# Query/key tiles as head pairs in every batch, and a new division into chunks

## The chip, the cores and the metric

One NeuronCore of a Trainium2 chip runs the whole program. The metric is the device time of one execution in microseconds, the median of several. The engines run side by side, each through its own instructions in order: PE (TensorE, matrix products, with PEld for its weight loads), DVE (VectorE), ACT (ScalarE), POOL (GpSimd) and SP (SyncE, whose queue issues the transfers). They wait for each other through semaphores.

## What is computed

Banded attention, then a feed-forward block, then a soft mixture of experts, all in float32. Shapes: q, k and v are 4 batches x 8 heads x 768 positions x 64; the rows that follow are 3072 x 512.

```python
def _attn_ref(q, k, v, n_global, n_local):          # 8 global keys, 96 local ones
    scores = scale * np.matmul(q, k.transpose(0, 1, 3, 2))
    ...
    scores = np.where(keep, scores + bias, -1e9)
    a = softmax(scores); return np.matmul(a, v)

def _moe_ref(x, w_in, w_out):                        # 512 -> 2048 -> 512
    h = x @ w_in
    return (h * (1.0 / (1.0 + np.exp(-h)))) @ w_out

def _moe2_ref(x, phi, w1, w2):                       # 8 experts, 4 slots each
    logits = x @ phi
    slot_input = softmax(logits, axis=0).T @ x
    ...
    return softmax(logits, axis=1) @ slot_out
```

## The kernel before

**Numbers in two halves.** Each float32 operand is split into a high and a low float16 part: `hi` (line 189) scales and rounds, `lo` (line 197) subtracts the high part from the input (lines 199 and 201 are its two forms). A product is then three: high x high, high x low, low x high.

**Tiles and chunks.** The 3072 rows are 24 tiles T of 128, six to a batch. `CHUNKS` (line 33) groups them, eight chunks of three. For a chunk c the feed-forward block runs as 16 calls of `l1_step` (line 453, 12 products of 384 columns each at lines 460 to 462, then Tanh on ACT at 464, a DVE multiply at 466 and the split of the result), and then `l2_part` and `l2_end` (lines 475 and 484, 48 products of 512 columns for each tile at lines 480 to 482, then the logits and the transposed copies). Behind a chunk follow `logits`, `slots1`, `slots2` and `slots3` (lines 497 to 555), the running softmax over all rows; L518, L528 and L548 are their products on PE. Each is put off by some slots with `at` (line 224): `lag_s` is 2.

**Attention.** `load(T)` (line 240) brings a tile's q, k and v through SP's queue into one staging buffer. `split(T)` (line 247) makes the halves: engine letters in `HE` and `HLO` choose who does it; from tile 6 on POOL does the high parts and DVE the low ones. `s_step(T, pr)` (line 272) takes heads 2pr and 2pr+1: scores on PE (line 293), mask and row maximum on DVE (298), exponential on ACT (299); after every second step the weights of four heads are split and transposed by a DMA (314). `pv_step(T, half)` (line 324) multiplies them by v (336) and scales (344 to 346).

There are two layouts for q and k, chosen by `paired(T)` (line 236), which is `T < NPAIR`, the first batch:
- Tiles 0 to 5 use `q_f` and `k_f`: 128 partitions hold two heads of 64, four such pairs side by side. The score of a head is three products over 64 rows, (high, high), (high, low), (low, high), and each head has its own PSUM bank. A split handles 128x512 elements.
- Tiles 6 to 23 use `q_l` and `k_l`: each head's 64 rows stand twice, one above the other, eight heads side by side. The high part of q stands in the upper 64 rows, its low part in the lower ones. A score is two products over 128 rows, with the high and with the low part of k. Both heads of a step share one bank, and the two banks of `bS` alternate from step to step. A split handles 128x1024 elements for k, and 64x1024 for the low part of q.

```python
h, r, terms = (pr, slice(64 * i, 64 * i + 64), ((0, 0), (0, 1), (1, 0))) if paired(T) else (2 * pr + i, slice(0, 128), ((0, 0), (0, 1)))
```

**Order.** `first_items` (line 358) runs the attention of chunk 0's tiles. After that chunk c's feed-forward work and the attention of chunk c+1 are interleaved: `other_items` (line 377) lists the attention calls, and `upto` marks how far a chunk must get. Each l1 step, and each quarter of a tile in l2, ends with `slot_end` (line 764), which runs the delayed work that is due and as many attention items as are proportional to the slots passed, over 16 + 4n - 5 slots for a chunk of n tiles. Chunk 0 has 28 slots in all and 29 items; it also carries the weight conversions `conv(p)` (line 414), eight for w_in ahead of the l1 steps that need them and eight for w_out in l2 (DVE at lines 421, 429, 430 and 448, ACT at 428 and 440, POOL at 426 and 446). A conversion's weights come through six places in SBUF, filled by `w_ahead` (line 407) on SP's queue when a place is free. The last chunk has no attention beside it and takes its own path (`last_part` and what follows), then come the expert layers and the output. The build sorts the instructions of an engine by when it expects them to be ready, so the order in the trace is near the code's but not the same.

Of the kernel before, what the change touches and what calls it, by code (L numbers as in the profile page):

```python
# [9 lines left out]
F32 = mybir.dt.float32  # L10
# [6 lines left out]
B, H, S, D = 4, 8, 768, 64  # L17
DM, DFF = 512, 2048
# [6 lines left out]
F16 = mybir.dt.float16  # L25
# [5 lines left out]
NTILE = NT // 128  # L31
TPB = S // 128
CHUNKS = [3, 3, 3, 3, 3, 3, 3, 3]
NCH = len(CHUNKS)
# [5 lines left out]
E_QK, E_V, E_WI, E_WO, E_G, E_X2, E_PHI, E_E = 0, 15, 16, 17, 14, 14, 13, 12  # L40
# [48 lines left out]
BE = 'A'  # L89
NPAIR = 6  # L90
HLO = 'VPVVVV'
# [8 lines left out]

def fast_kernel(tc, keepp, q_l, k_l, v_l, q_f, k_f, n_global, n_local, w_in, w_out, phi, w1, w2, shapes, pick_c, out):


    nc = tc.nc
    V, A, G = nc.vector, nc.scalar, nc.gpsimd
    mm = nc.tensor.matmul
# [3 lines left out]
    with ExitStack() as ctx:  # L110
# [4 lines left out]
        ar = Arena(pool.tile([128, NB // 4], F32, name="arena"), NB)  # L115
# [4 lines left out]
        bS, bPV, bW, bM = bank[0:2], bank[2], bank[3:7], bank[7]  # L120
# [38 lines left out]
        g0 = ar.off  # L159
# [75 lines left out]

        def paired(T):

            return T < NPAIR

        def load(T, bufs):  # L240
            if paired(T):
                bufs = [bufs[0][:, 0:4], bufs[1][:, 0:4], bufs[2]]
            for s, src in zip(bufs, (q_f, k_f, v_l) if paired(T) else (q_l, k_l, v_l)):
                nc.sync.dma_start(out=s, in_=src[T])
            staged[T] = bufs

        def split(T):
            qs, ks, vs = staged.pop(T)
            t, u = T % TPB, T % NR
            he = HE[T] if T < len(HE) else "P"  # L250
            le = HLO[T] if T < len(HLO) else "V"
            qd = q16[T % 2]
            n = 4 if paired(T) else 8
            if paired(T):
                qh, ql, qf = qd[:, 0:4], qd[:, 4:8], qs
            else:
                qh, ql, qf = qd, qd[64:128], qs[64:128]
            hi(he, qh, qs, E_QK)
            lo("P" if le == "P" else "V", ql, qf, E_QK, qh if paired(T) else ql)
            hi(he, kr[:, 0, 0:n, u], ks, E_QK)  # L260
            lo("V" if le == "V" else "P", kr[:, 1, 0:n, u], ks, E_QK, kr[:, 0, 0:n, u])
            v3 = vs.rearrange("p (h d) -> p h d", h=H)
            hi(he, v16[:, u, :, 0], v3, E_V)
            lo("V", v16[:, u, :, 1], v3, E_V, v16[:, u, :, 0])
            if t == 0:
                hi("P", kg[:, :, 0:n], kr[:, :, 0:n, u, 0:8], 0)
            if T == 0:
                hi("P", vg[0:8], v16[0:8, u], 0)
            if t == 2:
                absmax(T // TPB, v16[:, u, 0:2, 0], AX.XY)  # L270

        def s_step(T, pr):
            t, u = T % TPB, T % NR
            w = 128 if t == 0 else 256
            half, lp = pr // 2, pr % 2
            if paired(T):
                sp = [bS[i][:, 256 * (pr % 2):256 * (pr % 2) + 256] for i in range(2)]
            else:
                sp = [bS[pr % 2][:, 256 * i:256 * i + 256] for i in range(2)]
            pfb = pf[half]  # L280
            if t == 0 and T < C0 and PTE[2 * T + half] != "D":
                pfb = pfb.rearrange("p h c -> p (h c)")[:, 0:512].rearrange("p (h c) -> p h c", h=4)
            qd = q16[T % 2]
            for i in range(2):
                h, r, terms = (pr, slice(64 * i, 64 * i + 64), ((0, 0), (0, 1), (1, 0))) if paired(T) else (2 * pr + i, slice(0, 128), ((0, 0), (0, 1)))
                for j, (y, z) in enumerate(terms):
                    if t == 0:
                        kv = kr[r, z, h, u]
                    elif u > 0:
                        kv = kr[r, z, h, u - 1:u + 1]  # L290
                    else:
                        kv = kr[r, z, h, 0::NR - 1]
                    mm(sp[i][:, :w] if t == 0 else sp[i].rearrange("p (s c) -> p s c", s=2), qd[r, 4 * y + h], kv, start=(j == 0), stop=(j == len(terms) - 1))  # L293
            for i in range(2):
                h = 2 * pr + i
# [4 lines left out]
            if pr == 3 and 1 <= t < TPB - 1:  # L300
                n = 4 if paired(T) else 8
                hi("P", kr[:, :, 0:n, u, 0:8], kg[:, :, 0:n], 0)
            if lp == 1:
# [3 lines left out]
                if T < C0 and PTE[2 * T + half] != "D":  # L307
                    n = w // 32
# [7 lines left out]
                if T < C0:  # L316
                    done_p.add((T, half))
                    p = nload[0]
# [558 lines left out]
        i = NSMP  # L877
# [78 lines left out]
def dense_kernel(tc, q_l, k_l, v_l, n_global, n_local, w_in, w_out, phi, w1, w2, out):  # L956

    nc = tc.nc
    with ExitStack() as outer:
# [6 lines left out]
        with ExitStack() as ctx:  # L966
# [46 lines left out]
            for b in range(B):  # L1013
                x1t = one.tile([128, 4, S], F32, name="g_x1t")
                for h in range(H):
                    qs = wk.tile([64, S], F32, name="g_q")
                    nc.sync.dma_start(out=qs.rearrange("d (t s) -> d t s", t=6), in_=q_l[6 * b:6 * b + 6, 0:64, h].rearrange("t d s -> d t s"))
                    ks = wk.tile([64, S], F32, name="g_k")
                    nc.scalar.dma_start(out=ks.rearrange("d (t s) -> d t s", t=6), in_=k_l[6 * b:6 * b + 6, 0:64, h].rearrange("t d s -> d t s"))
                    vs = wk.tile([128, 6, D], F32, name="g_v")  # L1020
# [139 lines left out]

def tiles_of(np, a):

    a = a.reshape(B, H, TPB, 128, D).transpose(0, 2, 4, 1, 3).reshape(NTILE, D, H, 128)
    return np.concatenate([a, a], axis=1)


def pairs_of(a):

    return a[0].reshape(H // 2, 2, TPB, 128, D).transpose(2, 1, 4, 0, 3).reshape(TPB, 2 * D, H // 2, 128)

# [54 lines left out]
```

## Time and profile before

| | us |
|---|---|
| median of 3 runs | 767.23 (764.6 to 767.58) |
| the profiled execution's own time | 765.0 |
| its span, first to last instruction | 763.2 |

| engine | busy us | share | instructions |
|---|---|---|---|
| PE | 683.0 | 89% | 5559 |
| DVE | 489.0 | 64% | 1108 |
| ACT | 336.6 | 44% | 855 |
| POOL | 324.7 | 43% | 267 |

The durations of products overlap, since PE takes up the next one while the last still drains; what a product costs PE is the distance from start to start. A group of instructions that follow each other is one line of a timeline, with its count. The granted clock over the span is 0.964 of full speed. The stages, by the first product of each kind on PE: attention of tiles 0 to 2 and the first of tile 3 until 57.8 us; chunk 0 from 57.8 (l1) and 122.6 (l2) to 181.5; chunks 1 to 6 from 181.5 to 630, some 74.8 us each; the last chunk and the end from 630.

### The profile page before, as it was taken

To read this page: it belongs to the slowest core of one execution; us is meant where nothing else is said; L and a number is where in the kernel's file an instruction comes from. 1 tells how busy PE (TensorE), PEld (TensorE's weight loads), DVE (VectorE), ACT (ScalarE), POOL (GpSimd) and SP (SyncE) were. 2 spreads that over 40 slices of the span, in tenths; PEclk is the share of its full clock that TensorE was granted. 3 is DMA by queue.
4 is the path that set the end of the run, shared out by engine and by line. 5 is a ranking of instruction groups with operands and counts; after the bars stand their busy time and mean duration, and the time that the engine had idled before them with its cause. 6 is when DMAs were issued, how large, how long until landed. Compare 5 with 4: busy or idle time off the path is not lost.

```text
span 763.2 us, 14337 instructions
## 1 busy us (share of the span) xinstructions
PE 683.0 (89%) x5559; PEld 395.0 (52%) x5559; DVE 489.0 (64%) x1108; ACT 336.6 (44%) x855; POOL 324.7 (43%) x267
## 2 busy tenths in 40 slices
PE   2477757598999999999999999999999999998995
PEld 1244423244655565556556654665466546665375
DVE  6999999997775487548735873597266306505232
ACT  7756786553552255245423542454156305303122
POOL 4689684733455356415633673337324320101000
PEclk9978969799999999999999999999999999999997
DMA  6787645565456355733563567354532694295987
GB/s 237 194 249 205 218 87 152 191 181 120 75 125 139 83 113 137 174 75 77 132 138 74 107 137 167 56 111 109 86 43 43 150 320 178 97 357 214 391 330 223
DMA packets 162747, 120.22 MB, mean 158 GB/s; under 512 B 137456, under 2 KB 147184, under 8 KB 156656
## 3 DMA queue, kind: packets, MB, share of 16 engines
q1 hardware_dynamic: 162672, 119.23, 58.4%
q8 instruction: 45, 0.74, 0.4%
q14 instruction: 30, 0.25, 0.1%
HBM read 79.10 MB, written 6.29 MB: 112 GB/s over the span
## 4 chain that ended last, share of the span: by engine, by line
PE 67%; DVE 16%; issue 5%; POOL 4%; DMA 4%; ACT 3%; SPq 0%; ACTq 0%; DVEq 0%; POOLq 0%
PE bank L480 8%; PE bank L481 8%; PE bank L482 8%; PE bank L460 8%; PE bank L462 8%; PE bank L461 8%; PE bank L293 4%; PE bank L336 3%; DVE arena L201 2%; DMA arena<-arena 2%; DVE arena L199 2%; POOL arena L193 2%; PE bank L864 2%; DVE arena L429 2%; PE bank L902 2%
## 5 line engine op out<-in xcount | busy, mean ns | idle before, releaser
L193 POOL TENSOR_SCALAR arena<-arena 128x1024 f16<-128x1024 f32 (+5 forms) x146 | 144.4, 1002 | 237.0 <-ACT arena L299 102.5
L460 PE MATMUL bank<-rows,arena 128*128 128x384 f16 x512 | 168.4, 330 | 6.2 <-ACT arena L191 4.0
L462 PE MATMUL bank<-rows,arena 128*128 128x384 f16 x512 | 168.3, 329 | 0.8 <-DVE arena L448 0.8
L461 PE MATMUL bank<-rows,arena 128*128 128x384 f16 x512 | 168.3, 329 | 0.0
L191 ACT ACTIVATE arena<-bank 128x384 f16<-128x384 f32 (+2 forms) x165 | 81.8, 505 | 177.0 <-DVE bank L466 98.7
L199 POOL TENSOR_TENSOR arena<-arena 128x1024 f16<-128x1024 f32 (+2 forms) x69 | 131.0, 1900 | 41.3 <-ACT arena L191 37.3
L299 ACT ACTIVATE arena<-arena 128x256 f32<-128x256 f32 (+1 forms) x192 | 92.2, 482 | 98.2 <-DVE arena L298 95.3
L481 PE MATMUL bank<-arena 128*128 128x512 f16 x336 | 128.9, 384 | 2.7 <-POOL arena L446 1.9
L480 PE MATMUL bank<-arena 128*128 128x512 f16 x336 | 129.1, 384 | 1.5 <-DVE arena L201 1.5
L482 PE MATMUL bank<-arena 128*128 128x512 f16 x336 | 128.7, 383 | 0.0
L201 DVE SCALAR_TENSOR_TENSOR arena<-bank,arena 128x384 f16<-128x384 f32 (+2 forms) x142 | 81.3, 572 | 32.7 <-ACT arena L191 32.0
L293 PE MATMUL bank<-arena 128*128 128x256 f16 (+3 forms) x432 | 63.4, 288 | 41.5 <-DVE arena L298 23.9
L298 DVE CUSTOM_DVE_ANT_0 arena<-bank,arena 128x256 f32<-128x256 f32 (+1 forms) x192 | 70.5, 395 | 44.2 <-PE bank L293 42.8
L466 DVE SCALAR_TENSOR_TENSOR bank<-arena,bank 128x384 f32<-128x384 f32 x128 | 71.2, 557 | 31.0 <-ACT arena L464 29.8
L199 DVE TENSOR_TENSOR arena<-arena 128x1024 f16<-128x1024 f32 (+2 forms) x50 | 74.7, 1496 | 12.6 <-POOL arena L193 12.2
L464 ACT ACTIVATE arena<-bank 128x384 f32<-128x384 f32 x128 | 61.9, 484 | 21.1 <-PE bank L462 20.8
L293 PEld LDWEIGHTS <-arena 128*128 128x128 f16 (+1 forms) x432 | 36.3, 101 | 66.5 <-issue 38.1
L462 PEld LDWEIGHTS <-arena 128*128 128x128 f16 x512 | 50.4, 99 | 35.4 <-issue 1.6
L461 PEld LDWEIGHTS <-arena 128*128 128x128 f16 x512 | 50.4, 98 | 34.5 <-issue 7.2
L460 PEld LDWEIGHTS <-arena 128*128 128x128 f16 x512 | 50.5, 99 | 31.4 <-issue 2.9
L482 PEld LDWEIGHTS <-arena 128*128 128x128 f16 x336 | 33.1, 99 | 43.9 <-issue 5.3
L480 PEld LDWEIGHTS <-arena 128*128 128x128 f16 x336 | 33.2, 99 | 38.1 <-issue 4.8
(174 smaller groups left out, 808.8 us busy)
## 6 DMA issues: line engine op xcount, KB each, us to landing
arena<-in_w_dram SPq DMA_DIRECT2D x31, 1024.0 KB, 7.4
arena<-in_q_l_dram SPq DMA_DIRECT2D x18, 512.0 KB, 3.7
arena<-in_k_l_dram SPq DMA_DIRECT2D x18, 512.0 KB, 4.0
arena<-in_w_in_dram SPq DMA_DIRECT2D x8, 1024.0 KB, 5.7
arena<-in_w_out_dram SPq DMA_DIRECT2D x8, 1024.0 KB, 4.9
arena<-in_v_l_dram SPq DMA_DIRECT2D x24, 256.0 KB, 3.0
out_dram<-arena SPq DMA_DIRECT2D x4, 768.0 KB, 7.6
out_dram<-arena SPq DMA_DIRECT2D x8, 384.0 KB, 5.0
```

What stands on the lines that cost most here:

```text
L191: A.activation(out=out, in_=in_, func=AF.Copy, scale=p2(e))
L193: G.tensor_scalar(out=out, in0=in_, scalar1=p2(e), scalar2=0.0, op0=ALU.mult, op1=ALU.add)
L199: (V if eng == "V" else G).tensor_tensor(out=out, in0=in_, in1=h, op=ALU.subtract)
L201: V.scalar_tensor_tensor(out=out, in0=in_, scalar=p2(e), in1=h, op0=ALU.mult, op1=ALU.subtract)
L293: mm(sp[i][:, :w] if t == 0 else sp[i].rearrange("p (s c) -> p s c", s=2), qd[r, 4 * y + h], kv, start=(j == 0), stop=(j == len(terms) - 1))
L299: A.activation(out=pw, in_=pw, func=AF.Exp, scale=-1.0, bias=nmx[:, T, h:h + 1], accum_out=psum_[T % 2][:, h:h + 1])
L460: mm(hp, wh, x[:, 0, k], start=(k == 0), stop=False)
L461: mm(hp, wh, x[:, 1, k], start=False, stop=False)
L462: mm(hp, wl, x[:, 0, k], start=False, stop=(k == 3))
L480: mm(op, gh, woh[:, f, 0], start=(f == 0), stop=False)
L481: mm(op, gh, woh[:, f, 1], start=False, stop=False)
L482: mm(op, gl, woh[:, f, 0], start=False, stop=(f == 15))
```

## The change

All 24 tiles use the pair layout. `q_l` and `k_l` are now in it, `q_f`, `k_f`, `tiles_of`, `paired` and `NPAIR` are gone, and the buffers of q and k are half as large. In a step the three terms are the outer loop and the two heads the inner one, so the heads take turns. The chunks are 3, 2, 2, 2 and then five of 3 tiles: nine in place of eight, with chunk 0 and the last one as large as before. In chunk 0 the attention of chunk 1 is then that of two tiles (21 items); in chunk 3, which has two tiles of feed-forward work, that of three. The fallback for other masks reads the new layout; it doesn't run here.

```diff
-CHUNKS = [3, 3, 3, 3, 3, 3, 3, 3]
+CHUNKS = [3, 2, 2, 2, 3, 3, 3, 3, 3]
...
-NPAIR = 6
...
-        kr = ar.new([2, H, NR, 128], F16)
-        kg = ar.new([2, H, 8], F16)
-        q16 = [ar.new([H, 128], F16) for _ in range(2)]
+        kr = ar.new([2, H // 2, NR, 128], F16)
+        kg = ar.new([2, H // 2, 8], F16)
+        q16 = [ar.new([2, H // 2, 128], F16) for _ in range(2)]
...
-        stage_m = [ar.new([H, 128], F32), ar.new([H, 128], F32), ar.new([DM], F32)]
+        stage_m = [ar.new([H // 2, 128], F32), ar.new([H // 2, 128], F32), ar.new([DM], F32)]
...
-            for s, src in zip(bufs, (q_f, k_f, v_l) if paired(T) else (q_l, k_l, v_l)):
+            for s, src in zip(bufs, (q_l, k_l, v_l)):
...
-            hi(he, qh, qs, E_QK)
-            lo("P" if le == "P" else "V", ql, qf, E_QK, qh if paired(T) else ql)
-            hi(he, kr[:, 0, 0:n, u], ks, E_QK)
-            lo("V" if le == "V" else "P", kr[:, 1, 0:n, u], ks, E_QK, kr[:, 0, 0:n, u])
+            hi(he, qd[:, 0], qs, E_QK)
+            lo(le, qd[:, 1], qs, E_QK, qd[:, 0])
+            hi(he, kr[:, 0, :, u], ks, E_QK)
+            lo(le, kr[:, 1, :, u], ks, E_QK, kr[:, 0, :, u])
...
-            if paired(T):
-                sp = [bS[i][:, 256 * (pr % 2):256 * (pr % 2) + 256] for i in range(2)]
-            else:
-                sp = [bS[pr % 2][:, 256 * i:256 * i + 256] for i in range(2)]
+            sp = [bS[i][:, 256 * (pr % 2):256 * (pr % 2) + 256] for i in range(2)]
...
-            for i in range(2):
-                h, r, terms = (pr, slice(64 * i, 64 * i + 64), ((0, 0), (0, 1), (1, 0))) if paired(T) else (2 * pr + i, slice(0, 128), ((0, 0), (0, 1)))
-                for j, (y, z) in enumerate(terms):
+            for j, (y, z) in enumerate(((0, 0), (0, 1), (1, 0))):
+                for i in range(2):
+                    r = slice(64 * i, 64 * i + 64)
...
-            o = g0 + 10240 * (T - 1)
-            load(T, [ar.view(o, [H, 128], F32), ar.view(o + 4096, [H, 128], F32), ar.view(o + 8192, [DM], F32)])
+            o = g0 + 6144 * (T - 1)
+            load(T, [ar.view(o + 2048 * i, d, F32) for i, d in enumerate(([H // 2, 128], [H // 2, 128], [DM]))])
```

## Rows read from the trace of the kernel before

**Rows 1.** PE's line of the page's slices, 40 equal ones, busy tenths

```profile
PE   2477757598999999999999999999999999998995
```

**Rows 2.** Windows by stage: length, busy PE, PEld, DVE, ACT, POOL (instructions), clock, DMA

```profile
57.80:122.60 64.80, 47.23 (x319) 24.91 (x319) 63.66 (x80) 45.36 (x86) 48.14 (x31) 0.85 0.61 167
122.60:181.50 58.90, 43.68 (x249) 18.77 (x249) 54.92 (x73) 31.48 (x45) 28.83 (x18) 0.88 0.59 170
...
256.90:331.70 74.80, 73.51 (x616) 43.67 (x613) 49.58 (x125) 31.11 (x95) 38.83 (x32) 1.00 0.55 124
```

**Rows 3.** Timeline of PE in l2: start us, duration us, engine, line, operation

```profile
249.74 0.38 PE L481 MATMUL bank<-arena 128*128 128x512 f16 x1
...
253.84 0.38 PE L482 MATMUL bank<-arena 128*128 128x512 f16 x1
...
300.13 0.60 PE L293 MATMUL bank<-arena 128*128 128x256 f16 x4
300.56 0.38 PE L480 MATMUL bank<-arena 128*128 128x512 f16 x1
```

**Rows 4.** Timeline of PE around a 64-row step in chunk 0

```profile
75.27 0.33 PE L462 MATMUL bank<-rows,arena 128*128 128x384 f16 x1
...
75.76 0.33 PE L462 MATMUL bank<-rows,arena 128*128 128x384 f16 x1
76.02 0.51 PE L293 MATMUL bank<-arena 64*128 64x256 f16 x6
76.46 0.59 PE L423 MATMUL bank<-arena 128*1 128x512 bf16 x2
```

**Rows 5.** Timeline of PE at a chunk's third slot step

```profile
282.10 1.03 PE L548 MATMUL bank<-arena 128*128 128x32 f16 x35 [1.29 <-DVE arena L201]
```

**Rows 6.** Timeline of PE, a step of a batch's first tile

```profile
333.68 0.39 PE L293 MATMUL bank<-arena 128*128 128x128 f16 x4
333.90 0.33 PE L460 MATMUL bank<-rows,arena 128*128 128x384 f16 x1
```

**Rows 7.** Timeline of PE, half a tile's weights-times-values products

```profile
263.67 0.86 PE L336 MATMUL bank<-arena 128*128 128x64 f16 x24
264.37 0.33 PE L460 MATMUL bank<-rows,arena 128*128 128x384 f16 x1
```

**Rows 8.** Groups by line and shape, whole span: count | busy us, mean ns | idle before

```profile
L298 DVE CUSTOM_DVE_ANT_0 arena<-bank,arena 128x256 f32<-128x256 f32 x160 | 62.3, 417 | 30.5 <-PE bank L293 29.1 <-POOL arena L193 1.1
...
L346 DVE TENSOR_TENSOR arena<-bank,arena 128x512 f32<-128x512 f32 x24 | 16.5, 687 | 5.1 <-PE bank L336 5.1
...
L298 DVE CUSTOM_DVE_ANT_0 arena<-bank,arena 128x128 f32<-128x128 f32 x32 | 8.2, 284 | 13.7 <-PE bank L293 13.7
...
L528 PE MATMUL bank<-arena 96*128 96x96 f32 x14 | 2.5, 260 | 0.0
```

**Rows 9.** Groups by line and shape, DVE in chunk 0

```profile
L199 DVE TENSOR_TENSOR arena<-arena 128x1024 f16<-128x1024 f32 x6 | 11.9, 1991 | 0.7 <-POOL arena L193 0.7
...
L199 DVE TENSOR_TENSOR arena<-arena 64x1024 f16<-64x1024 f32 x2 | 4.8, 2392 | 0.1
...
L199 DVE TENSOR_TENSOR arena<-arena 128x512 f16<-128x512 f32 x3 | 2.0, 679 | 0.0
```

**Rows 10.** Timeline of DVE, then of POOL, in chunk 0

```profile
74.50 2.11 DVE L344 TENSOR_SCALAR arena<-arena 128x8 f32<-128x8 f32 x1
...
73.49 3.10 POOL L446 TENSOR_TENSOR arena<-arena 128x1024 f16<-128x1024 f32 x1
```

**Rows 11.** Groups by line and shape, POOL in chunk 0

```profile
L193 POOL TENSOR_SCALAR arena<-arena 128x1024 f16<-128x1024 f32 x9 | 13.9, 1543 | 1.1 <-ACT arena L299 1.0
```

**Rows 12.** Timeline of DVE in a later chunk

```profile
265.87 1.21 DVE L199 TENSOR_TENSOR arena<-arena 128x1024 f16<-128x1024 f32 x1
```

**Rows 13.** Chain that ended last, in time order, chunk 0: start us, us, what

```profile
160.74 5.33 DMA arena<-in_w_out_dram
```

**Rows 14.** Timeline of PE, another 64-row step in chunk 0

```profile
91.10 0.83 PE L293 MATMUL bank<-arena 64*128 64x256 f16 x6 [0.67 <-DVE arena L298]
```

More of the change, by code (lines that the diff above doesn't have):

```diff
@@ L98, with fast_kernel @@
 CTE = "AAAVVVVV"
-def fast_kernel(tc, keepp, q_l, k_l, v_l, q_f, k_f, n_global, n_local, w_in, w_out, phi, w1, w2, shapes, pick_c, out):
+def fast_kernel(tc, keepp, q_l, k_l, v_l, n_global, n_local, w_in, w_out, phi, w1, w2, shapes, pick_c, out):
     nc = tc.nc
@@ L265, in split @@
             if t == 0:
-                hi("P", kg[:, :, 0:n], kr[:, :, 0:n, u, 0:8], 0)
+                hi("P", kg, kr[:, :, :, u, 0:8], 0)
             if T == 0:
@@ L283, in s_step @@
             qd = q16[T % 2]
-            for i in range(2):
-                h, r, terms = (pr, slice(64 * i, 64 * i + 64), ((0, 0), (0, 1), (1, 0))) if paired(T) else (2 * pr + i, slice(0, 128), ((0, 0), (0, 1)))
-                for j, (y, z) in enumerate(terms):
+            for j, (y, z) in enumerate(((0, 0), (0, 1), (1, 0))):
+                for i in range(2):
+                    r = slice(64 * i, 64 * i + 64)
                     if t == 0:
-                        kv = kr[r, z, h, u]
+                        kv = kr[r, z, pr, u]
                     elif u > 0:
-                        kv = kr[r, z, h, u - 1:u + 1]
+                        kv = kr[r, z, pr, u - 1:u + 1]
                     else:
-                        kv = kr[r, z, h, 0::NR - 1]
-                    mm(sp[i][:, :w] if t == 0 else sp[i].rearrange("p (s c) -> p s c", s=2), qd[r, 4 * y + h], kv, start=(j == 0), stop=(j == len(terms) - 1))
+                        kv = kr[r, z, pr, 0::NR - 1]
+                    mm(sp[i][:, :w] if t == 0 else sp[i].rearrange("p (s c) -> p s c", s=2), qd[r, y, pr], kv, start=(j == 0), stop=(j == 2))
             for i in range(2):
@@ L300, in s_step @@
             if pr == 3 and 1 <= t < TPB - 1:
-                n = 4 if paired(T) else 8
-                hi("P", kr[:, :, 0:n, u, 0:8], kg[:, :, 0:n], 0)
+                hi("P", kr[:, :, :, u, 0:8], kg, 0)
             if lp == 1:
@@ L1016, in dense_kernel @@
                     qs = wk.tile([64, S], F32, name="g_q")
-                    nc.sync.dma_start(out=qs.rearrange("d (t s) -> d t s", t=6), in_=q_l[6 * b:6 * b + 6, 0:64, h].rearrange("t d s -> d t s"))
+                    nc.sync.dma_start(out=qs.rearrange("d (t s) -> d t s", t=6), in_=q_l[6 * b:6 * b + 6, 64 * (h % 2):64 * (h % 2) + 64, h // 2].rearrange("t d s -> d t s"))
                     ks = wk.tile([64, S], F32, name="g_k")
-                    nc.scalar.dma_start(out=ks.rearrange("d (t s) -> d t s", t=6), in_=k_l[6 * b:6 * b + 6, 0:64, h].rearrange("t d s -> d t s"))
+                    nc.scalar.dma_start(out=ks.rearrange("d (t s) -> d t s", t=6), in_=k_l[6 * b:6 * b + 6, 64 * (h % 2):64 * (h % 2) + 64, h // 2].rearrange("t d s -> d t s"))
                     vs = wk.tile([128, 6, D], F32, name="g_v")
@@ L1158, in dense_kernel @@
                 nc.sync.dma_start(out=out[r * 128:r * 128 + 128], in_=o)
-def tiles_of(np, a):
-    a = a.reshape(B, H, TPB, 128, D).transpose(0, 2, 4, 1, 3).reshape(NTILE, D, H, 128)
-    return np.concatenate([a, a], axis=1)
 def pairs_of(a):
-    return a[0].reshape(H // 2, 2, TPB, 128, D).transpose(2, 1, 4, 0, 3).reshape(TPB, 2 * D, H // 2, 128)
+    return a.reshape(B, H // 2, 2, TPB, 128, D).transpose(0, 3, 2, 5, 1, 4).reshape(NTILE, 2 * D, H // 2, 128)
 def kernel(**inputs):
@@ L1179 @@
     laid = {
-        "q_l": tiles_of(_np, inputs["q"]),
-        "k_l": tiles_of(_np, inputs["k"]),
-        "q_f": pairs_of(inputs["q"]),
-        "k_f": pairs_of(inputs["k"]),
+        "q_l": pairs_of(inputs["q"]),
+        "k_l": pairs_of(inputs["k"]),
         "v_l": inputs["v"].transpose(0, 2, 1, 3).reshape(NTILE, 128, H * D),
@@ L1218 @@
                 ok = nc.values_load(flag[0:1, 0:1])
-                for name in ("shapes", "pick_c", "q_f", "k_f"):
+                for name in ("shapes", "pick_c"):
                     del args[name]
```

9 lines of the change are left out of this document (removed).

## The prediction

> **What bounds the kernel now.** I read the slices first, then the windows by stage, then PE's timeline in two stages. The slices [rows 1] show two regimes: PE is partly idle in the first nine or so of forty slices and full from there on. The windows [rows 2] put numbers on it. In chunk 0 (57.8 to 181.5 us: the first l1 and l2, with the weight conversions between) VectorE is busy 63.66 of 64.80 and 54.92 of 58.90 us, 118.6 of 123.7 together, while PE has a quarter to spare. In a later chunk (256.9 to 331.7) it is the other way round: PE 73.51 of 74.80, DVE 49.58, POOL 38.83. There PE is bound by its pace from start to start: nineteen steps of l2 products take 4.10 us, 0.2155 each [rows 3], three of l1 products 0.49, 0.163 each [rows 4]. 144 of the one and 192 of the other are 62.3 us of the 74.8; attention, logits and slots fill the rest but for a bubble of 1.29 us [rows 5]. So a nanosecond of PE added behind 181.5 us is paid in full, and one added in chunk 0 hardly counts; for DVE it is the reverse.
>
> **Part 1: one pair step on PE.** A tile has four steps; tiles 0 to 5 have the pair form already, so 18 tiles change, from four 128-row products per step to six 64-row ones. Neither form has to be guessed. A 128-row step in the stream hands on to the next product 0.43 to 0.44 after its start [rows 3]: four products at 0.109, no edge. A 64-row step [rows 4] runs its two heads side by side: six products are through in 0.51, where the last one's own duration, 0.27, is included. But it starts 0.26 after the l1 product ahead of it, where the pace is 0.163, and the next instruction comes 0.44 after its start, of which three products are 0.33. So entry and exit cost some 0.10 each. From pace to pace: 0.095 + 0.44 against 0.44, that is **0.095 us more per step**, though one product's time is won.
> The Trainium skill, TensorEngine Tiling (Array Packing), sections Theoretical Speedup and Performance Considerations, says that with a contraction of 64 or less row tiling goes up to twice as fast. By that alone a step would take 0.33 and the sum would come out 15 us lower. The same page, section Key Properties, says that a change of the tiling mode drains TensorE; the 0.10 at each edge agrees with that.
> Fifteen of the 18 tiles have the full width: 60 x 0.095 = 5.7. The first tile of a batch has 128 columns: 0.22 now [rows 6], against an estimate of 0.095 + 3 x 0.055 + 0.095 = 0.355 from these rows; 12 x 0.135 = 1.6. Its bounds are 0.095 and 0.17 per step; I take the one nearer to the two measured edges. **Part 1 is +7.3**, all of it where PE is full.
>
> **Part 2: the chunks, on PE.** Both versions have three tiles in chunk 0 and in the last chunk, and 18 tiles between, as six chunks now and seven then (2, 2, 2, 3, 3, 3, 3). What leaves chunk 0 is by the code eight items (21 stay of 29): s_step(5, 3), s_step(6, 0 to 2), both halves of pv_step(5), split(7), load(8). On PE they go from a stage with room into the full one: 0.53 + 3 x 0.22 + 2 x 0.70 [rows 7] = +2.6 (the narrow steps' surcharge is in Part 1). Three l1 at 256 columns cost 3 x 192 x 0.109 = 62.8 against 2 x 192 x 0.163 = 62.6; that products of 256 with fresh weights keep 0.109 is in [rows 3]. +0.2. One chunk more brings one round more of slots1 to slots3: the bubble of 1.29 [rows 5] and small products, some 0.36 by L528's 2.5 us in seven chunks [rows 8]. +1.7. **Part 2 is +4.5**; Parts 1 and 2 are +11.8.
>
> **Part 3: waits that grow.** slots1, slots2 and slots3 stand two slots apart, and slots3 (L548) waits 1.29 us for DVE even now [rows 5]; on PE all l1 products queue behind it. A slot in l1 is 12 x 0.163 and some 0.6 of attention, 2.5 us; with two tiles 12 x 0.109 + 0.6 = 1.9. So at the starts of chunks 1, 2 and 3 each lead is 1.2 us shorter, and the DVE chain within hardly so. That is 1.2 if slots3 alone waits and 2.4 if slots2 does too, 3.6 to 7.2 in all; below that 0, if DVE answers sooner for its halved splits. I take **+5**: the wait is there already, so a shorter lead shows. DVE's and ACT's l1 work shrinks with the columns (417 ns for 256, 284 for 128 in L298 [rows 8]), about as the slot does.
>
> **Part 4: chunk 0 gets shorter.** DVE sets its length, so what leaves DVE counts. Eight wide subtractions of line 199 lie there: six of 128x1024, 11.9 us, and two of 64x1024, 4.8 [rows 9]. Six of the eight are low parts of queries and keys, which become 128x512 at 0.68 [rows 9]; of the two others (weights of tile 5) one moves out. 6 x 0.68 + 2.0 = 6.1 remain: -10.6. The moved items take 2 x 0.42 + 6 x 0.28 of L298 and 0.69 of L346 with them [rows 8]: -3.2. So -14, if DVE is the bound all through.
> Those durations hold waiting. L344, eight columns, took 2.11 us while POOL's L446 ran from 73.49 to 76.59 [rows 10]. POOL work that leaves (its 128x1024 copies take 1543 ns each [rows 11], and those of queries and keys become half as wide) thus gives DVE time too: up to -20. From the other side, a 128x1024 subtraction in a quieter stretch takes 1.21 [rows 12], so the six splits may be worth 3.2 only, and something else may hold the end of the chunk: -4. Near 160 us the chain runs through a load of w_out, 5.33 us [rows 13], that waited in SP's queue behind a transpose for POOL. I take **-12**, nearest to the DVE sum, since DVE is busy 96% of the chunk.
> Transfers: 36 loads halve, by the code from 512 to 256 KB, all on SP's queue; behind chunk 0 PE never waits for them, so nothing. The prologue (tiles 0 to 2) has its form already; that its products now take the heads by turns costs nothing there, with PE half idle.
>
> **Sum.** 11.8 + 5 - 12 = +5. The profiled execution took 765.0 (span 763.2): 770. The median of the three runs is 767.2, or 2.2 more: **772**.
>
> **Rivals.** (a) Chunk 0 gives 20, POOL's relief on top, and the slots wait 1 us more in all: 11.8 + 1 - 20 = -7, **760**, faster. For it: [rows 10]. Against it: [rows 13]. It decides once chunk 0 ends before 165 us.
> (b) Pair steps without their edges, 3 x 0.11: 73 steps at 0.20 less than in the sum, 5 - 14.6 = -10, **758**. It could come from steps that stand next to each other; [rows 4] speaks against it.
> (c) Chunk 0 gives 15 and the slots wait 3: 0, **767**, no change; the DVE sum taken whole.
> (d) More waits, **780**. A step now has one bank for its two heads and takes the banks by turns; a pair step writes both, so it waits for the reads of the step just before it. One such step waited 0.67 for L298 in chunk 0 [rows 14]. Chunk 3 has 24 attention items in 19 slots, where a chunk of three has 23: 12 steps x 0.67 = 8 us. Against it: the halved splits make DVE less late. Chunk 0 giving only 4 ends at the same 780.
>
> **How the numbers follow.** Forecast 0.40, of which 0.12 lie below 771; (a) 0.17, (b) 0.07, (c) 0.20, (d) 0.16. A measurement of this kernel tells about 0.5%, 3.8 us, from no change: below 763.4 is faster, above 771.1 slower. Faster 0.17 + 0.07 = 0.24; same 0.20 + 0.12 = 0.32; slower 0.28 + 0.16 = 0.44. The range takes in (b) and (a) below and (d) above, 758 to 782; the forecast's own is 768 to 777.
>
> **What would show it.** Pair steps behind chunk 0 that start 0.26 after the last l1 product and hand on after 0.44, else Part 1 is wrong. A chunk of three near 76.0 us, where it is 74.8, and one of two near 52. Chunk 1's first product near 169.5 instead of 181.5: before 165 it is (a), after 177 the weak end of Part 4. Idle PE ahead of L528 and L548 of some 2.5 us at three chunk starts. The wide low parts of line 199 gone from DVE's groups. Idle PE ahead of L293 for L298 of over 5 us in chunk 3: (d).

## The result, and the profile after

The changed kernel takes **771.87 us** (median of 5 runs, 770.24 to 772.54) against 767.23 (764.60 to 768.38): a ratio of 1.0062, 95% interval 1.0042 to 1.0081. It is slower by 0.6 per cent, a little over the half per cent that can be told here; the forecast was 772. The profiled execution took 770.83, its span 769.0 where that of before was 763.2: +5.8.

Where the 5.8 us lie is read from the first product of each stage, in one profiled execution of each kernel:

| stage, us | before | after | difference |
|---|---|---|---|
| ahead of the first l1 product | 57.8 | 64.0 | +6.2 |
| chunk 0 | 123.7 | 108.5 | -15.2 |
| the chunks between (six, seven) | 448.4 | 464.6 | +16.1 |
| last chunk and experts | 133.2 | 131.9 | -1.3 |

The chunks between took 75.4, 74.8, 74.7, 74.8, 74.7 and 74.2 us; now they take 51.8, 52.6, **61.7**, 74.3, 75.3, 75.1 and 74.0.

The windows by stage answer to [rows 2], with the same columns: chunk 0 in its two parts, the third chunk of two tiles, and a chunk of three.

```profile
64.00:119.60 55.60, 44.09 (x276) 23.15 (x276) 54.02 (x66) 43.36 (x75) 36.70 (x22) 0.90 0.45 131
119.60:172.50 52.90, 41.49 (x225) 17.51 (x225) 40.60 (x60) 27.36 (x36) 16.47 (x15) 0.95 0.52 154
276.85:338.50 61.65, 57.89 (x566) 38.11 (x563) 37.21 (x121) 27.42 (x92) 33.48 (x32) 0.94 0.56 117
412.80:488.00 75.20, 74.93 (x637) 41.27 (x634) 45.50 (x125) 31.36 (x95) 33.00 (x32) 1.00 0.44 99
```

VectorE no longer fills chunk 0's second part (40.6 of 52.9 us). In the chunk of three PE is busy 74.93 of 75.20 us, where 1.29 us stood idle in [rows 2]. The chunk in the third line has idle PE again, and a clock of 0.94 of full speed.

A pair step among l1 products, from PE's timeline behind chunk 0; it answers to [rows 4]. The third and fourth lines are a narrow step (a batch's first tile), which answers to [rows 6].

```profile
414.55 0.33 PE L449 MATMUL bank<-rows,arena 128*128 128x384 f16 x1
414.80 0.50 PE L281 MATMUL bank<-arena 64*128 64x256 f16 x6
415.24 0.34 PE L447 MATMUL bank<-rows,arena 128*128 128x384 f16 x1
...
340.29 0.33 PE L449 MATMUL bank<-rows,arena 128*128 128x384 f16 x1
340.54 0.34 PE L281 MATMUL bank<-arena 64*128 64x128 f16 x6
340.82 0.34 PE L447 MATMUL bank<-rows,arena 128*128 128x384 f16 x1
```

The wide step starts 0.25 us after the last l1 product and hands on 0.44 after its start, as the prediction had it; the narrow one starts after 0.25 and hands on after 0.28, that is 0.15 more than the 0.22 of [rows 6].

PE's waits in the third chunk of two (engine, line, releaser: us in total, times, longest), then PE's timeline at the longest of them, then POOL's at that time:

```profile
PE bank L281 <- POOL arena L194: 2.6, 1, 2.6
PE bank L281 <- DVE arena L286: 0.9, 3, 0.4
```

```profile
292.93 0.27 PE L449 MATMUL bank<-rows,arena 128*128 128x256 f16 x1
295.79 0.76 PE L281 MATMUL bank<-arena 64*128 64x256 f16 x3 [2.59 <-POOL arena L194]
296.48 0.40 PE L447 MATMUL bank<-rows,arena 128*128 128x256 f16 x1
296.67 0.42 PE L448 MATMUL bank<-rows,arena 128*128 128x256 f16 x1
```

```profile
293.58 1.29 POOL L200 TENSOR_TENSOR arena<-arena 128x512 f16<-128x512 f32 x1 [0.48 <-ACT arena L192]
294.85 1.68 POOL L194 TENSOR_SCALAR arena<-arena 128x512 f16<-128x512 f32 x4
```

PE sits idle for 2.59 us ahead of a step, which starts at 295.79 us, while POOL is among four copies of line 194. Behind the wait the l1 products start some 0.2 us apart instead of 0.11. The windows ahead of it and behind it show why: the granted clock (the number after the last bracket) is 1.00 and then 0.53, about the lower of its two levels (1.2 and 2.4 GHz), for 7 us. From 303 us on it is full again.

```profile
285.00:295.00 10.00, 8.07 (x92) 6.41 (x91) 8.12 (x29) 7.01 (x23) 6.19 (x6) 1.00 0.54 102
295.50:302.50 7.00, 6.71 (x49) 4.39 (x49) 5.65 (x17) 2.96 (x10) 4.24 (x5) 0.53 0.46 89
```

PE is busy almost all of these 7.0 us; at 0.53 of the speed they cost an estimated 3.3 us. With 2.6 us of waiting for POOL and 0.9 for DVE that is 6.8 us in one chunk, more than the whole difference between the two kernels.

### The profile page after: what moved, and what is told of

Read it like the earlier page. It is cut to its first block, busy times and chain, and to the rows that moved or that the text cites. A ratio compares the mean times of both kernels' runs of the same rounds, so it can differ in the third digit from the quotient of the medians.

```text
span 769.0 us, 15106 instructions
## 1 busy us (share of the span) xinstructions
PE 695.9 (90%) x5898; PEld 400.0 (52%) x5898; DVE 460.2 (60%) x1152; ACT 341.2 (44%) x889; POOL 287.6 (37%) x267
## 4 chain that ended last, share of the span: by engine, by line
PE 67%; DVE 17%; ACT 7%; issue 3%; POOL 3%; DMA 2%; SPq 0%; ACTq 0%; DVEq 0%; POOLq 0%
PE bank L447 8%; PE bank L467 8%; PE bank L469 8%; PE bank L468 8%; PE bank L449 8%; PE bank L448 8%; PE bank L281 4%; DVE arena L417 3%; PE bank L323 3%; DVE arena L416 3%; PE bank L851 2%; DVE bank L453 2%; DVE arena L202 2%; PE bank L889 2%; ACT arena L415 2%
## 5 line engine op out<-in xcount | busy, mean ns | idle before, releaser
L194 POOL TENSOR_SCALAR arena<-arena 128x512 f16<-128x512 f32 (+4 forms) x146 | 115.8, 807 | 284.8 <-ACT arena L287 113.8
L447 PE MATMUL bank<-rows,arena 128*128 128x384 f16 (+1 forms) x576 | 180.9, 315 | 3.6 <-ACT arena L192 2.3
L448 PE MATMUL bank<-rows,arena 128*128 128x384 f16 (+1 forms) x576 | 180.2, 313 | 0.0
L449 PE MATMUL bank<-rows,arena 128*128 128x384 f16 (+1 forms) x576 | 180.1, 313 | 0.0
L192 ACT ACTIVATE arena<-bank 128x384 f16<-128x384 f32 (+3 forms) x181 | 84.8, 477 | 194.1 <-DVE bank L453 97.8
L200 POOL TENSOR_TENSOR arena<-arena 128x1024 f16<-128x1024 f32 (+2 forms) x69 | 125.6, 1822 | 32.2 <-ACT arena L192 28.1
L453 DVE SCALAR_TENSOR_TENSOR bank<-arena,bank 128x384 f32<-128x384 f32 (+1 forms) x144 | 74.2, 516 | 40.9 <-ACT arena L451 40.1
L281 PE MATMUL bank<-arena 64*128 64x256 f16 (+1 forms) x576 | 57.5, 283 | 35.7 <-DVE arena L286 20.9
L447 PEld LDWEIGHTS <-arena 128*128 128x128 f16 x576 | 56.9, 99 | 37.6 <-issue 14.6
L451 ACT ACTIVATE arena<-bank 128x384 f32<-128x384 f32 (+1 forms) x144 | 64.5, 449 | 26.1 <-PE bank L449 25.8
L449 PEld LDWEIGHTS <-arena 128*128 128x128 f16 x576 | 57.2, 99 | 28.4 <-issue 1.7
L448 PEld LDWEIGHTS <-arena 128*128 128x128 f16 x576 | 57.1, 99 | 27.9 <-issue 5.8
L281 PEld LDWEIGHTS <-arena 64*128 64x128 f16 x576 | 25.2, 98 | 68.5 <-issue 53.8
L467 PEld LDWEIGHTS <-arena 128*128 128x128 f16 x336 | 33.0, 98 | 42.3 <-issue 8.0
L469 PEld LDWEIGHTS <-arena 128*128 128x128 f16 x336 | 33.1, 99 | 40.3 <-issue 1.1
L200 DVE TENSOR_TENSOR arena<-arena 128x512 f16<-128x512 f32 (+1 forms) x50 | 46.2, 931 | 11.0 <-POOL arena L194 10.9
```

Source lines behind the costliest of these rows:

```text
L447: mm(hp, wh, x[:, 0, k], start=(k == 0), stop=False)
L448: mm(hp, wh, x[:, 1, k], start=False, stop=False)
L449: mm(hp, wl, x[:, 0, k], start=False, stop=(k == 3))
L453: V.scalar_tensor_tensor(out=hp, in0=th, scalar=1.0, in1=hp, op0=ALU.add, op1=ALU.mult)
L467: mm(op, gh, woh[:, f, 0], start=(f == 0), stop=False)
L469: mm(op, gl, woh[:, f, 0], start=False, stop=(f == 15))
```

## The experiments

Each ratio compares an experiment's runs with runs of the kernel before on the same chip. The medians of before lie between 765.3 and 767.5 us there, so ratios, not microseconds, compare one experiment with another. Starts and ends of stages come from one profiled execution of each kernel.

**The pair form alone, and the chunks alone.** Two edits take the change apart:

```diff
 # pairs_only, against the changed kernel
-CHUNKS = [3, 2, 2, 2, 3, 3, 3, 3, 3]
+CHUNKS = [3, 3, 3, 3, 3, 3, 3, 3]
 # chunks_only, against the kernel before
-CHUNKS = [3, 3, 3, 3, 3, 3, 3, 3]
+CHUNKS = [3, 2, 2, 2, 3, 3, 3, 3, 3]
```

> The changed kernel with eight chunks of three: the pair form alone. Theory 1 (the pair form lightens DVE, and a lighter DVE answers the slots in time): the steps' edges cost 0.095 x 60 + 0.135 x 12 = +7.3 us behind chunk 0; chunk 0 loses its six wide low parts, 8 to 10 us; the bubble of 1.3 us ahead of the slots' last products, there in six chunks before, falls to about 0.2: -7. In all 767.2 + 7.3 - 9 - 7 = 758 to 760 us. Theory 2 (the bubble went because the order of the chunks changed): six bubbles of 1.3 us stay, and the time is 765 to 767 us. Rival (chunk 0 got shorter only because items were moved out of it): its end stays near 181 us, and the time is 768 to 775 us.

> The kernel before with the new chunks: the other half alone. By the sum: moved items +2.6 and one more chunk +1.9 on PE behind chunk 0, nothing for edges; chunk 0 gives 3.2 us of moved DVE work and one wide split, so some 5 to 7. Theory 1 (DVE is the slots' releaser, and its wide low parts stay): the bubble stays in every chunk and grows where the chunk before it has two tiles, by 1.2 to 2.4 us each: 767.2 + 4.5 + 4 - 6 = 769 to 772 us. Theory 2 (the new order itself removes the bubble): 7 less, 760 to 763 us. If the two halves of the change add up, this one and the pairs alone lie together 4.6 us above twice the kernel before.

| | time, us | ratio, 95% | first l1 product | end of chunk 0 | chunks between |
|---|---|---|---|---|---|
| before | 766.78 | | 57.8 | 181.5 | 448.4 |
| pairs only | 769.41 | 1.0035, 1.0021 to 1.0049 | 57.4 | 178.8 | 459.2 |
| chunks only | 776.57 | 1.0133, 1.0116 to 1.0150 | 63.6 | 172.4 | 467.0 |
| both | 771.87 | 1.0062, 1.0042 to 1.0081 | 64.0 | 172.5 | 464.6 |

The halves don't add up: 0.35 and 1.33 per cent make 1.68, and the two together cost 0.62, some 8 us less. By the profiles they fail to add up behind chunk 0: the chunks between grew by 10.8 and 18.6 us by themselves, and by 16.1 together. Four things follow.

First, the earlier end of chunk 0 comes from the new chunks. The pair form brings it forward by 2.8 us alone and by nothing on top of the new chunks. The windows of the pairs alone, chunk 0's two parts:

```profile
57.40:122.40 65.00, 47.41 (x318) 24.76 (x317) 62.05 (x87) 46.23 (x86) 44.83 (x31) 0.87 0.60 169
122.40:178.80 56.40, 44.93 (x256) 18.82 (x256) 47.43 (x69) 30.09 (x44) 24.99 (x18) 0.88 0.54 159
```

DVE's busy time fell from 118.6 us [rows 2] to 109.5, but the chunk from 123.7 to 121.4 only: of 9.1 us taken off the engine that was busy 96%, some 7 became idle time.

Second, the later start of l1 (+6.2) comes from them as well.

Third, it is the pair form that removes the bubble of [rows 5], as theory 1 says. In the four middle chunks of the pairs alone PE waits 0.3 us or less for DVE; with the chunks alone the bubble is still there in a chunk of three. That a lighter DVE is the reason is theory 1's argument; the pair form also halves copies of POOL and the loads, and no run separates these. PE's waits, chunks only, first in the third chunk of two and then in a chunk of three:

```profile
PE bank L293 <- POOL arena L193: 3.6, 1, 3.6
PE bank L336 <- DMA arena<-arena: 3.6, 2, 2.5
PE bank L528 <- DVE arena L521: 1.4, 1, 1.4
...
PE bank L548 <- DVE arena L201: 1.5, 1, 1.5
```

The edges, too, are seen there: in two middle chunks of the pairs alone PE is busy 75.01 and 74.66 us where it was 73.49 and 73.38. Over all six chunks the difference is 7.4 us (448.5 against 441.0), read from pairs_load below, which also has the pair form in chunks of three and whose clock is full in each of the six.

Fourth, the crowded chunk (the third of two tiles) comes from the new chunks: 64.8 us with the chunks alone, 61.7 with both. The pair form, whose splits are half as wide, relieves it. The pairs alone lose 3.0 us each in the first and the last chunk between for transposes, which the changed kernel hardly does (0.7 and 0.2). Their profiled execution took 774.06 us, 4.7 over the median; in pairs_load, profiled close to its median, these waits are 3.1 and 1.5, so the second may be above the usual. The profiled execution of the chunks alone took 773.34, 3.2 under its median, and shows less than is lost on the average.

**POOL's high parts in the crowded chunk moved to ACT**, against the changed kernel:

```diff
-HE = 'AVPPPA'
+HE = 'AVPPPAPPPAAAA'
```

> The changed kernel, with the high parts of queries, keys and values of tiles 9 to 12 on ACT in place of POOL. Theory (the third chunk of two came some 6 us long because attention waited for POOL's high part of the keys, 2.6 us, and the clock then stood at its lower level for some 7 us; the chunk before it lost 1.8 us at the same place): both waits go, the clock stays up, and the time falls by 5 to 8 us to 764 to 767. Rival (24 attention items in 19 slots are too dense whoever makes the high part; another wait takes its place, or ACT becomes late with the exponentials): 770 to 774 us, with PE idle for as long in the same stretch.

It took 770.80 us, 1.0048 (1.0034 to 1.0062) of before. By the ratios that is 1 us less than the changed kernel, and the two intervals overlap: a miss. PE's waits show the same releaser, 1.2 us in the second chunk of two and 2.2 in the third. Below them stand POOL's and PE's timelines at the longer one:

```profile
PE bank L281 <- POOL arena L194: 1.2, 1, 1.2
...
PE bank L281 <- POOL arena L194: 2.2, 1, 2.2
PE bank L323 <- DMA arena<-arena: 0.7, 1, 0.7
PE bank L281 <- DVE arena L286: 0.7, 2, 0.4
```

```profile
296.38 0.32 POOL L194 TENSOR_SCALAR arena<-arena 128x64 f16<-128x64 f16 x1
...
296.75 0.38 PE L281 MATMUL bank<-arena 64*128 64x256 f16 x2 [2.22 <-POOL arena L194]
```

The copies that were moved are gone from there, and the step still waits, for a small copy of the same line, 128x64: it ends at 296.70 us and the step starts at 296.75. By the code it is that of the global keys (issued at line 289), which follows a tile's last step and precedes the next tile's first. It stands in POOL's queue behind the low part of the attention output, and that one waits for ACT. In the changed kernel the same small copy is among the four above (295.43 to 295.74 us). So the theory named the wrong copy.

**One item more between those two steps**, against the changed kernel. The first try, step_between, moved the last step of a tile ahead of pv_step(T - 1, 1):

> The changed kernel, from tile 6 on with the last step of a tile one item earlier, so that half an attention product (pv_step) stands between it and the first step of the next tile. Where POOL sets the first eight keys of the tile to the global ones, it does so behind the tile's last step, and the next tile's first step waits for it. Theory (in the second and third chunk of two these two steps come closer together than POOL needs, since there are more attention items than slots; the 2.6 us of idle PE then bring the lower clock): the two waits on POOL's line 194 go, chunks 2 and 3 take 51 and 56 to 57 us in place of 52.6 and 61.7, and the time is 764 to 767 us. Rival (the crowd itself costs, whatever stands next to what; PE then waits at another place, for the transposes or for DVE): 770 us or more, chunk 3 still over 60 us.

```diff
                 items.append(lambda T=T: s_step(T, 2))
+                if T > 5:
+                    items.append(lambda T=T: s_step(T, 3))
...
-                items.append(lambda T=T: s_step(T, 3))
+                if T <= 5:
+                    items.append(lambda T=T: s_step(T, 3))
```

That step fills the buffer from which pv_step(T - 1, 1) reads, so this kernel multiplies the values of one tile with the attention weights of the next, and it has to wait for those. Its 834.64 us say nothing on the theory. The second try moves the other neighbour:

```diff
             for T in range(C0, NTILE):
+                if T > 6:
+                    items.append(lambda T=T: pv_step(T - 1, 0))
                 items.append(lambda T=T: s_step(T, 0))
-                if T > C0:
+                if C0 < T <= 6:
```

> The changed kernel, from tile 7 on with the first half attention product of the tile before (pv_step) ahead of the tile's first step instead of behind it, so that one item more stands between a tile's last step and the next tile's first. Theory (the next tile's first step waits for POOL's copy of the global keys, which stands in POOL's queue behind other copies; the items come closer than that where 24 stand in 19 slots): an item is worth 1.6 us there, so the waits of 1.8 and 2.6 us for POOL's line 194 fall below 1 us each, the clock stays at its upper level in chunk 3, and chunk 3 takes 57 to 58 us in place of 61.7: 765 to 768 us. Rival (the crowd itself costs): the idle time turns up ahead of the half products, for the transposes, or for DVE, chunk 3 stays over 60 us and the time within 1.5 us of 771.9.

777.00 us, 1.0147 (1.0130 to 1.0164): the theory falls. The rival is right on the place and wrong on the time, which is over 5 us above the 771.9 that it named. The waits for POOL's line 194 are gone from the chunks between, and others stand in their place, in the first two chunks of two as well (53.4 and 54.1 us where the changed kernel takes 51.8 and 52.6). PE's waits in the third chunk of two, which now takes 62.8 us:

```profile
PE bank L323 <- DVE arena L286: 3.3, 1, 3.3
PE bank L281 <- DVE arena L286: 1.7, 1, 1.7
PE bank L323 <- POOL rows L200: 1.0, 1, 1.0
PE bank L323 <- DMA arena<-arena: 0.6, 1, 0.6
```

So in the four kernels with the new chunks (step_between aside) the third chunk of two comes long, 60.4 to 64.8 us, with different releasers. That its 24 attention items in 19 slots are the cause fits this, but isn't shown: a version of the new chunks that spreads these items wasn't tried. The count alone doesn't order the waits, since the second chunk of two, with 16 items in 19 slots, waits 1.8 us and the chunks of three, with 24 in 23, hardly at all (changed kernel).

**Pairs in two batches**, against the kernel before (NPAIR is 12, and the pair arrays hold two batches):

> The kernel before with pairs in the first two batches (tiles 0 to 11) in place of the first, chunks of three as they were. Theory (what the pair form gives lies in chunk 0, what it costs lies behind it): 20 full-width steps at 0.095 and 4 narrow ones at 0.135 cost 2.4 us; the splits in chunk 0 are all halved, 8 to 10 us; the bubble goes in the one or two chunks whose splits are halved: 767.2 + 2.4 - 9 - 2 = 757 to 760 us. Rival (chunk 0's end is held by the loads of the weights, not by DVE): 767 to 770 us.

769.57 us, 1.0037 (1.0022 to 1.0051): a miss, with the time in the rival's range. Chunk 0 ends at 177.3 us, not near 172, and the first chunk behind it waits 4.5 us for transposes (0.8 before). The bubble goes where the attention beside a chunk has the pair form (0.4 us in the second chunk between, 1.3 before) and stays in the next three (1.3, 1.5 and 1.3).

**The last weight load on another queue**, against the kernel before and against the pairs alone (pairs_load):

```diff
-                nc.sync.dma_start(out=ar.view(place[p], [2048], I32), in_=(w_in if p < 8 else w_out)[p % 8].bitcast(I32))
+                (nc.scalar if p == 15 else nc.sync).dma_start(out=ar.view(place[p], [2048], I32), in_=(w_in if p < 8 else w_out)[p % 8].bitcast(I32))
```

> The kernel before with the last of the weight loads on ACT's queue in place of SP's, where it stands behind two transposes that wait for POOL. Theory (the end of chunk 0 hangs on this load, so the halved splits of the pair form cannot bring it forward, and the moved items of the new chunks can, because the transposes then stand behind the load): chunk 0 ends 4 to 8 us earlier than 181.5 us with everything else as it was, and the time falls to 759 to 763 us. Rival (DVE's sum holds the end, as the prediction had it): DVE has the same work, the end stays within 2 us of 181.5 and the time within 2 us of 767.

> The pair form with eight chunks of three, and the last weight load on ACT's queue. The pair form alone brought the end of chunk 0 forward by 2.8 us and the load alone by 2.1. Theory (two chains end chunk 0 at nearly the same time, DVE's and that of the load behind the transposes; each hides what the other gives): together they give more than the sum of 4.9, 7 to 10 us, the end comes at 172 to 175 us, and the time is 4 to 5 us under that of the pairs alone, 764 to 766 us. Rival (a third chain ends just before, the conversions' chain between ACT and DVE): the end at 177 us or later, and 768 us or more.

The first: 765.97 us, 0.9990 (0.9977 to 1.0002), chunk 0's end at 179.4. The second: 769.60, 1.0046 (1.0028 to 1.0065), its end still at 178.8. Both theories fall. The reason for trying was this stretch of the chain that ended last, in the pairs alone, where the load (that of [rows 13]) stands behind a transpose on SP's queue and that behind POOL:

```profile
152.33 1.69 POOL arena L194
...
154.10 2.02 POOL arena L200
...
156.13 1.24 SPq L301
...
157.47 5.66 DMA arena<-in_w_out_dram
...
163.15 2.51 ACT arena L415
```

With the load out of the way something else ends less than 3 us earlier. In the first of the two runs it is DVE, as the prediction had it for the kernel before: DVE is busy 119.2 of the chunk's 121.7 us, and its lines make up most of the chain. In the second DVE is busy 109.4 of 121.4 us only, and the end stays. What ends the chunk in the changed kernel, the chain of that kernel shows: the last conversions of weights go between ACT and DVE, one after the other.

```profile
149.68 2.40 ACT arena L415
...
152.11 1.33 DVE arena L416
...
153.46 1.23 DVE arena L417
...
156.23 1.13 ACT arena L427
157.36 2.40 ACT arena L415
```

Line 415 of the last three conversions starts at 143.47, 149.68 and 157.36 us: 6.2 us apart, and 7.7 with an attention step between. DVE has only 2.6 us of such a round; ACT's next line 415 is queued behind its line 427 of the round before. I didn't take this chain apart by an experiment.

**The price of an edge by itself.** The kernel before with one useless product per l1 step (its result is overwritten), of 64 rows and, as a control, of 128:

```diff
             x, g = xt[c], g_of[CHUNKS[c]]
+            mm(hp[:, 0:128], ident16[0:64], ident16[0:64, 0:128], start=True, stop=True)
```

> The kernel before with one useless product of 64 rows and 128 columns ahead of the 12 products of every l1 step (its result is overwritten). Theory (what a pair step pays is the change between 64 and 128 rows, 0.095 us into it and as much out of it): 0.055 for the product and 0.19 for the two edges, 0.245 x 112 steps in the chunks that PE sets = 27 us, 794 us in all. Rival (the edge comes from something else in a pair step, such as its two banks or its own weight loads): 0.055 to 0.1 each, 6 to 11 us, 773 to 778 us, as with a product of 128 rows.

> The control of the 64-row product: the same useless product with 128 rows. Theory and rival both: 0.055 us, perhaps 0.1 with its weight load, times 112 steps = 6 to 11 us, 773 to 778 us. If it costs as much as the 64-row product, the edge isn't the rows.

789.77 us against 771.54 (two runs each): the theory holds. Over 112 steps the difference is 18.2 us, 0.16 each; both totals lie below what was expected, by 4 us and by 1.5. PE's timelines, 64 rows first, then 128:

```profile
262.80 0.60 PE L293 MATMUL bank<-arena 128*128 128x256 f16 x4
263.33 0.23 PE L458 MATMUL bank<-arena 64*128 64x128 f16 x1
263.49 0.34 PE L461 MATMUL bank<-rows,arena 128*128 128x384 f16 x1
```

```profile
261.02 0.60 PE L293 MATMUL bank<-arena 128*128 128x256 f16 x4
261.46 0.22 PE L458 MATMUL bank<-arena 128*128 128x128 f16 x1
261.52 0.33 PE L461 MATMUL bank<-rows,arena 128*128 128x384 f16 x1
```

Entry 0.53 against 0.44 after the product group ahead, exit 0.16 against 0.06: 0.09 and 0.10, so the edge is the number of rows. The windows of one chunk say the same, PE busy 77.60 against 74.40 us, 0.20 for each of 16. The total gives 0.04 less each, 4 us in all. Most of that is waiting that the longer chunks no longer have: PE waits 4.6 us in the six chunks of the control and 1.3 in those with 64 rows.

**The lead of the slots**, against the kernel before, alone and with the load on ACT's queue (lag3_load):

```diff
-CFG = dict(phi="P", plo="P", xhi="A", xlo="P", ghi="A", lag_l=5, lag_s=2, tail_slots=5)
+CFG = dict(phi="P", plo="P", xhi="A", xlo="P", ghi="A", lag_l=5, lag_s=3, tail_slots=5)
```

> The kernel before with the steps of the slots (slots1 to slots3) three slots apart in place of two. Theory (the bubble ahead of the slots' last products, 1.3 us in four chunks, is a lead that is too short by that much; the pair form removed it by making DVE answer sooner): a slot is 2.5 us, so the bubble goes altogether, and the time falls by 4 to 6 us to 761 to 763. Rival (DVE has its work in order and comes to these steps later as well, or the later steps collide with the second product stage): the bubble stays or moves, and the time is within 1.5 us of 767.

> The kernel before with the slots' steps three slots apart and the last weight load on ACT's queue: the two edits that took time away. Theory (the first works behind chunk 0, the second at its end, so they add up): 0.9977 x 0.999 = 0.9967 of the kernel before, 763 to 764 us by its median of 766 to 767; chunk 0 ends near 179.5 us and chunks of three take 73.2 to 75.5. Rival (both act on DVE's order, which a program arranges anew for each kernel): within 1 us of the later slots alone, 0.9977.

Alone 763.31 us, 0.9977 (0.9962 to 0.9993); with the load **762.72**, 0.9942 (0.9924 to 0.9961), the one version that is faster than the kernel before by more than half a per cent. The two medians lie 0.6 us apart, and most of the difference between the ratios is in the runs of before, 765.33 and 767.46, so what the load adds isn't settled. With the later slots alone, in the chunk at 332 us PE's wait is gone and the chunk takes 73.2 us instead of 74.7; in the one ahead of it a new wait stands (the first line below) and it takes 75.4 instead of 74.8, so nearly half of the gain is given back.

```profile
PE bank L293 <- POOL arena L193: 1.2, 1, 1.2
PE bank L548 <- DVE arena L201: 0.5, 1, 0.5
```

## Why the prediction was right, and where it wasn't

**Part 1, the pair steps, was right in place and nearly in size.** Forecast: a start after 0.26, a hand-on after 0.44, 0.095 more per step, +7.3 in all. The steps show 0.25 and 0.44 among l1 products; the narrow step cost 0.15 more where 0.135 was estimated; by PE's busy time six chunks pay 7.4 us. The control with 64 and 128 rows shows that the edge belongs to the rows, 0.09 and 0.10 us. The Trainium skill, TensorEngine Tiling (Array Packing), section Key Properties, says that changing the tiling mode drains TensorE; this pair of runs agrees, and gives the price. Rival (b), steps without edges, is out.

**Part 2, the chunks on PE, was right in what a chunk of two costs.** The first takes 51.8 us with 1.0 of waiting, the second 52.6 with 1.8; "near 52" was forecast. Its bubble for one more round of slots didn't come.

**Part 3, waits that grow, was wrong in its reason.** The slots' waits didn't grow to 2.5 us at three chunk starts; they are 0.4, 0 and 0 us there, and the bubble of [rows 5] all but went from the chunks of three too. The step that failed is "the wait is there already, so a shorter lead shows": the same paragraph named the other side, DVE answering sooner for its halved splits, as the lower bound, and that is what came: the bubble stays with the chunks alone and goes with the pair form. A chunk of three takes 74.0 to 75.3 us for that, not 76.0. In its place came 1.8 us in the second chunk of two and 6.8 in the third, 3.3 of them the clock's. The place is the one that rival (d) gave, chunk 3 with 24 items in 19 slots, and its price is near; the releaser isn't, since PE waits 0.9 us there for DVE, not over 5. Once POOL's wait is removed, DVE's comes up (1.7 and 3.3 us), so the engine at the end of the wait is exchangeable; that the density of items is the cause is argued, not shown. Nothing in the prediction priced the 3.3 us that the lower clock adds behind such a wait.

**Part 4, a shorter chunk 0, was near by a wrong sum.** Forecast -12, measured -9.0 at the end of the chunk: -15.2 in it and +6.2 ahead of it. The working went by DVE: 10.6 us for halved low parts and 3.2 for moved items (the low parts of split(7), which is moved too, were left in). DVE's busy time fell by even more, from 118.6 to 94.6 us, and still the end came only 9.0 us earlier. The pair form alone, which has all of the halved parts and none of the moved items, gave 2.8. The step that failed is "I take -12, nearest to the DVE sum, since DVE is busy 96% of the chunk". The bound on the other side, -4 for the halved parts because something else may hold the end, was the better one for them; what the moved items brought was underrated. They take with them attention steps and transposes that stood in the queues between the conversions; whether that is the reason, and which of them counts most, wasn't tested.

The prologue was taken as unchanged, and that step failed too. "Costs nothing there", said of the heads that take turns, held: with the pairs alone l1 starts at 57.4 us. The new list of chunks moved the start by 6.2. The prologue's items are the same, but the program's build arranges each engine's order anew. DVE's timelines before (first) and after, ahead of the first l1 step, where the attention output of tile 2 (lines 346 and 333) is what l1 waits for:

```profile
54.14 1.30 DVE L429 TENSOR_SCALAR arena<-arena 128x1024 uint16<-128x1024 uint16 x1
55.23 0.72 DVE L346 TENSOR_TENSOR arena<-bank,arena 128x512 f32<-128x512 f32 x1
55.88 1.52 DVE L430 SCALAR_TENSOR_TENSOR arena<-arena 128x1024 int32<-128x1024 int32 x1
```

```profile
54.30 3.35 DVE L416 TENSOR_SCALAR arena<-arena 128x1024 uint16<-128x1024 uint16 x2
57.46 3.13 DVE L417 SCALAR_TENSOR_TENSOR arena<-arena 128x1024 int32<-128x1024 int32 x1
60.51 0.68 DVE L333 TENSOR_TENSOR arena<-bank,arena 128x512 f32<-128x512 f32 x1
```

One more step of line 416, and a slow line 417, now stand ahead of it, and PE waits 4.4 us. That conversion is then missing from chunk 0 (12 steps of line 416 where there were 13 of line 429), so part of this is a shift rather than a loss.

**The sum.** The total came out partly by luck. Behind chunk 0 16.8 us (11.8 + 5) were forecast and 16.1 measured, but by other terms. PE's busy time there rose by 16.0, from 441.0 to 457.0 us: 7.4 are the pair steps', 3.3 the clock's, and 5.3 are left for the moved items, the extra chunk and short waits that overlapping records hide, where Part 2 had 3.2 without its bubble. PE's idle time there hardly changed, from 7.4 to 7.5 us, where the bubble and Part 3 together added 6.3: what the slots' waits and the transposes gave back, the crowded chunks took. The clock's term, which was not forecast, and 2.1 us more of work filled most of that gap. Of Part 4's -12 came -9.0, and the last stage, of which nothing was said, gave 1.3 of the missing 3. Rivals (a) and (c), which needed 15 to 20 us from chunk 0, are out: its end came 9 us earlier.

## What to carry to other kernels

An edge that each instruction group pays on the engine that sets the time can be summed from two rows of a timeline, and holds to about a tenth. A busy share of 96% doesn't make all of an engine's work a stage's length: of 9.1 us taken off it, 2.3 were gained, because something else ended just behind; ask what ends next before a whole sum is booked. Where work units are spread over slots, look at the fullest stretch: the wait that shows there may be only the first of several. Here one edit against the named releaser gained no more than 1 us, and another, which removed its wait, brought the next ones and cost some 6.

## What the runs showed of the hardware that was not expected

A wait of 2.6 us of PE was followed by 7.0 us at a granted clock of 0.53, an estimated 3.3 us lost, more than the wait itself; in the same kernel a wait of 1.8 us in the chunk before left the clock of that chunk at 1.00. DVE's line 417, which takes 1.23 us in a quiet stretch (at 153.46), took 3.13 at 57.46, while POOL's line 200 ran from 56.58 to 59.51. And the pair form, whose two heads run side by side, saves PE no time in this kernel: from the last l1 product to the next, a wide step takes 0.25 + 0.44 us where four products of 128 rows took 0.16 + 0.44.
